# Another load order and other priorities for a fused retention and squared-ReLU FFN kernel

## The chip, the cores and the metric

The kernel runs on one core of a Trainium2 chip. The metric is the device time of one execution in microseconds. Before the change three runs gave 211.70, 212.27 and 212.51 us, so a median of 212.27 us; the profiled execution has a span of 210.5 us from its first to its last instruction.

The names of the engines: PE is TensorE (PEld its weight loads), DVE is VectorE, ACT is ScalarE, POOL is GpSimd, SP is SyncE, which issues nearly all DMAs here.

## The reference, cut to what matters

There are 4 sequences of 768 tokens, 8 heads of 64. A retention recurrence is run over q, k and v, and its output, laid out as 3072 tokens of 512 features, goes through an FFN with 2048 hidden units and a squared ReLU.

```python
gamma = 1.0 - 2.0 ** (-5.0 - np.arange(H))
scale = 1.0 / np.sqrt(D)
for t in range(S):
    state = gamma[None, :, None, None] * state + np.einsum('bhd,bhe->bhde', k[:, :, t], v[:, :, t])
    y[:, :, t] = scale * np.einsum('bhd,bhde->bhe', q[:, :, t], state)
...
x = y.transpose(0, 2, 1, 3).reshape(B * S, H * D)      # 3072 x 512
h = np.maximum(x @ w_in, 0.0)                          # w_in 512 x 2048
return h * h @ w_out                                   # w_out 2048 x 512
```

Inputs and output are float32. The kernel computes the matmuls in bfloat16 with float32 sums.

## The kernel before

The tokens are worked on as 24 tiles of 128. The recurrence is done in chunks: masked scores of a chunk with itself, plus the state of the chunks before, which is carried in bfloat16 and updated by a sum per chunk. The first four tiles are done as two **pairs** (tiles 0 and 1, tiles 2 and 3), whose q, k and v are loaded with 256 tokens each; the later tiles have loads of their own.

The program is not written in the order in which it is issued. Every operation (a load, a cast, a group of matmuls, an eviction) is first added to a `Plan` with its engine, an assumed duration, what it reads and writes, and a priority. Then the plan is run as a list schedule: of all operations whose inputs are there, the one that can start first is placed, and of those that can start at the same time the one with the lowest priority number. The order found so is fixed in the program; the chip keeps to it on each engine and waits where the model was wrong.

```python
best = None
for eng, cand in pool.items():
    for i in cand:
        t = max(eng_free[eng], ready_at[i])
        ...                                    # PSUM banks
        key = (t, o["prio"], i)
        if best is None or key < best[0]:
            best = (key, i, eng)
```

The model of a load has a pipe with a cost per load[...]:

```python
RING = 198; FETCH = 2.6; BLOCK0 = 193; BLOCK = 256; AHEAD = 50      # of class Plan
...
if any(before < x <= issued for x in range(self.BLOCK0 - self.AHEAD, issued + 1, self.BLOCK)):
    behind = [x for x in moves if x[0] > t + 0.4]
    y = max(behind[0][1] if behind else pipe, t + 0.4) + 1.27
    ...                                        # the loads behind it land later
```

The parameters that the plan takes (cut to those that the text speaks of):

```python
SMALL = (1.20, 0.93, 65, 0.6)    # load of a tile: ..., descriptors 65
TWIN = (1.20, 1.80, 65, 0.6)     # load of a pair
BLOCKS = [2, 2, 1, 1, 2, 2, 2, 4, 4, 4]     # tiles in a block of the FFN's first matmul
AHEAD = 4        # how many tiles ahead the loads and casts are added to the plan
WARM = 20.0      # fill matmuls are put in gaps of TensorE up to about this time
PACE = 5; LEAD = 2
NPE = 6; NTD = 7 # tiles 6 to NTD - 1 are turned with 64 x 64 transposes on TensorE, later ones by DMA
PRE = 20         # tiny matmuls at the very start
WHALF = 2        # the first two quarters of w_in come in halves: pieces i0 to i3; then i4, i5
F2LAG = 4.0; F2WAIT = 4
HOME = {...}     # operations that are tied to one engine
RANK = {...}     # priorities set by hand
ORDER = "k0 q0 v0 q2 k2 i0 v2 o0 k4 i1 o1 ..."
```

In the list of loads, `k2` is the k of the tile (or pair) that begins with tile 2, `i0` the first piece of w_in, `o0` the first of w_out. The place in the list is the priority of the load:

```python
dma_prio = {x: n for n, x in enumerate(dma_order(NM))}
```

The weights are loaded as float32 into four staging buffers and cast to bfloat16 from there; w_in and w_out share them, and the pieces of w_in are added to the plan before those of w_out:

```python
pieces = {"in": [(j, h, 2) for j in range(WHALF) for h in range(2)] + [(j, 0, 1) for j in range(WHALF, 4)],
          "out": [(j, 0, 1) for j in range(4)]}

def weights(kind, n):
    j, half, parts = pieces[kind][n]
    slot = (j if kind == "in" else 4 + j) % NWS            # NWS = 4
    ...
    held = [f"wst{slot}.{half}"] if parts == 2 else [f"wst{slot}.0", f"wst{slot}.1"]
    pl.add(f"ldw{kind}{n}", "SP", WHALFD if parts == 2 else WIDE, (), held, ..., prio=dma_prio[(kind, n)])
    for c in range(0, 4, parts):
        pl.add(f"cw{kind}{n}.{c}", WCAST, 0, held, [...], ..., prio=WPRIO[kind] + j)
```

A pair is loaded, cast (`c`), its v scaled (`cv`, on VectorE or GpSimd, line 452), turned (`T`, `E`), scored (`A`, masked by `P`), summed into the state (`B`, line 512, `S`) and applied (`C`, lines 522 and 533; `Y` writes the result to `xt`). B of a pair waits for both halves of its scaled v. Later tiles have `visit(m, n)`, which applies tile m and scores tile n in one group (lines 686, 701, 712, 723). Its priority on TensorE:

```python
prio=-300 + n if m is None else -300 + m if m < PACE else (m - LEAD) * 8
```

The FFN's first matmul (line 835), relu and square (lines 840 and 845), and second matmul (line 880):

```python
pl.add(f"F1.{blk}.{f0}", "PE", ..., prio=blk0[blk] * 8 + 2 * f0 * nb / 4, ...)
pl.add(f"F2.{q4}.{j}",   "PE", ..., prio=(q4 + F2LAG) * 8 + 2 * j + 1 + part * 9, ...)
```

A tile is turned on TensorE or by a DMA transpose (line 660):

```python
if m < 2 * NPAIR or NPE <= m < NTD:
    return                                       # flips(t) in a visit: line 642, then one eviction on ScalarE
if m >= NPE:
    pl.add(f"X{m}", "SP", TURN, ..., lambda: nc.sync.dma_start_transpose(...), prio=-0.5)
    return
```

At the very start and in early gaps TensorE is given work without use[...]:

```python
for _ in range(PRE):
    nc.tensor.matmul(fps[NBANK - 1][0:1, 0:1], lhsT=one, rhs=one, start=True, stop=True)          # line 932
for i in sequence:
    for _ in range(o.get("fill", 0)):
        nc.tensor.matmul(fps[o["fill_bank"]][:, 0 : 2 * P], lhsT=ident[:], rhs=..., ...)          # line 936
```

Of the kernel before, what the change touches and what calls it, by code (L numbers as in the profile page):

```python
# [18 lines left out]
class Plan:  # L19
# [12 lines left out]
    BLOCK = 256  # L32
    AHEAD = 50
    HOP = 0.15
# [6 lines left out]
    def add(self, name, eng, dur, reads=(), writes=(), fn=None, prio=0.0, lat=0.0, bank=None, after=(), count=0):  # L41
# [17 lines left out]
        else:  # L59
            flex = True  # L60
        if name in HOME:
            eng = {HOME[name]: eng[HOME[name]]}
        prio = RANK.get(name, prio)
        self.ops.append(dict(i=i, name=name, eng=eng, flex=flex, deps=sorted(deps), fn=fn,
# [3 lines left out]
    def schedule(self, nbanks, max_open):  # L68
# [18 lines left out]
        if "PE" in eng_free:  # L87
            eng_free["PE"] = 0.06 * PRE
        bank_free = [0.0] * nbanks
# [7 lines left out]
        done = 0  # L97
        issued, edge, next_fetched, history, crossed = 2 * PRE, self.BLOCK0, 3.0, [], 0.0
        while done < n:
# [54 lines left out]
            else:  # L154
                if eng == "PE":
# [9 lines left out]
                    while issued + todo > edge:  # L165
                        step = max(0, edge - issued)
                        now = max(now + step * per, next_fetched)
                        issued, todo = max(issued, edge), todo - step
                        ahead = next((y for x, y in reversed(history) if x <= edge - self.AHEAD), 0.0)
                        ahead = max(ahead, crossed)  # L170
# [5 lines left out]
                    history.append((issued, t + dur))  # L176
                    if any(before < x <= issued for x in range(self.BLOCK0 - self.AHEAD, issued + 1, self.BLOCK)):
                        behind = [x for x in moves if x[0] > t + 0.4]
# [37 lines left out]
STORE = (0.30, 0.80, 9, 0.6)  # L216
BLOCKS = [2, 2, 1, 1, 2, 2, 2, 4, 4, 4]
SPLIT = 6
AHEAD = 4
WARM = 20.0  # L220
FILL = 0.215
WARMING = 18.4
PACE = 5
LEAD = 2
NPE = 6
NTD = 7
PRE = 20
WHALF = 2
WHALFD = (0.60, 1.47, 33, 0.6)
CVT = {'DVE': 0.69, 'POOL': 1.3}  # L230
TCAST = {'DVE': 0.43, 'ACT': 0.63, 'POOL': 0.78}
TEVAC = {'ACT': 0.6, 'DVE': 0.62}
NPAIR = 2
F2LAG = 4.0
F2WAIT = 4
LAST = [256, 128, 128]
CAST = {"k": {"DVE": 0.43, "ACT": 0.63, "POOL": 0.78}, "q": {"DVE": 0.43, "ACT": 0.63, "POOL": 0.78}}
# [2 lines left out]
WPRIO = {"in": -2.0, "out": 2.0}  # L240


HOME = {'cq2.1': 'POOL', 'Eq2.0': 'DVE', 'cq0.1': 'ACT', 'cwout3.3': 'ACT', 'cwin2.0': 'DVE', 'cwin0.0': 'ACT', 'ck2.0': 'ACT', 'ck5': 'DVE', 'Eq4': 'DVE', 'Eq0.1': 'ACT', 'cq4': 'ACT', 'cwin1.2': 'ACT', 'ck6': 'DVE', 'Ek0.0': 'DVE', 'cwout2.3': 'DVE', 'cwin1.0': 'ACT', 'cwin3.2': 'DVE', 'Ek4': 'ACT', 'cwout0.3': 'DVE', 'cq0.0': 'DVE', 'ck4': 'POOL', 'cwin5.2': 'ACT', 'cwout0.1': 'DVE', 'cwout3.1': 'DVE', 'cwout1.3': 'DVE', 'cwout1.0': 'DVE', 'cwout0.2': 'DVE'}
ROUND = []
RANK = {'Ek0.0': -98.1}
ORDER = (
    "k0 q0 v0 q2 k2 i0 v2 o0 k4 i1 o1 i2 q4 o2 i3 o3 i4 v4 i5 q5 q6 q7 k5 v5 v6 k6 k7 v7"
)


# [8 lines left out]
def kernel(  # L259
# [346 lines left out]
    def prepare(m):  # L606
        if m < 2 * NPAIR:
            if m % 2 == 0:
                together(m // 2)
            return  # L610
        b, i = where(m)
        slot = m % NLD
        for x in "kqv":
            t = ld[x][:, slot, :]
            pl.add(f"ld{x}{m}", "SP", SMALL, (), (f"ld{x}{slot}",),
                   lambda x=x, t=t: nc.sync.dma_start(  # L616
                       t.rearrange("s (h d) -> s h d", h=H),
                       src[x][b, :, i * C : (i + 1) * C, :].rearrange("h s d -> s h d")),
                   prio=dma_prio[(x, m)])
        for x in "kq":  # L620
            t, o = ld[x][:, slot, :], bf[x][m % NBF]
            pl.add(f"c{x}{m}", CAST[x], 0, (f"ld{x}{slot}",), (f"bf{x}{m % NBF}",),
                   lambda on, t=t, o=o: copy_on(on, o.rearrange("s j a d -> s a j d"),
                                                t.rearrange("s (a j d) -> s a j d", a=2, j=NJ)), prio=urgency(m))
        t, o = ld["v"][:, slot, :], bf["v"][m % NBF]
        pl.add(f"cv{m}", "DVE", 0.69, (f"ldv{slot}", "vf"), (f"bfv{m % NBF}",),
               lambda: nc.vector.tensor_tensor(  # L627
                   out=o[:], in0=t.rearrange("s (h d) -> s h d", h=H),
                   in1=vf[:, i, :, None].to_broadcast([P, H, D]), op=ALU.mult),
               prio=urgency(m))  # L630
# [21 lines left out]
    def transpose(m):  # L652


        qkT, t = qkts[m % NQT], kq[m % NBF]
# [3 lines that stand above are left out]
            pl.add(f"X{m}", "SP", TURN, (f"bfk{m % NBF}", f"bfq{m % NBF}"), qkeys(m),  # L659
                   lambda: nc.sync.dma_start_transpose(out=qkT.rearrange("p x j t -> p (x j) t"),  # L660
                                                       in_=t.rearrange("s x j a d -> s (x j a d)")), prio=-0.5)
            return
        for x, name in enumerate("kq"):
            o1 = {}

            def fn(x=x, o1=o1):
                ps = fps[o1["op"]["bank_index"]].bitcast(BF16)
                for j in range(NJ):
                    nc.tensor.transpose(ps[:, j * P : j * P + P], t[:, x, j].rearrange("s a d -> s (a d)"), ident[:])
            i0 = pl.add(f"T{name}{m}", "PE", 0.26, (f"bf{name}{m % NBF}", "ident"), (f"gT{name}{m}",), fn,  # L670
                        prio=-200 + m, lat=0.2, count=4, bank=("open", ("T", m, x), False))
            o1["op"] = pl.ops[i0]
            pl.add(f"E{name}{m}", EVAC, 0, (f"gT{name}{m}",), (qkeys(m)[x],),
                   lambda on, x=x, o1=o1: copy_on(on, qkT[:, x].rearrange("p j t -> p (j t)"),
                                                  fps[o1["op"]["bank_index"]].bitcast(BF16)[:, 0:512]),
                   prio=urgency(m), lat=0.05, bank=("close", ("T", m, x)))
# [50 lines left out]
    def visit(m, n, t=None):  # L727
# [28 lines left out]
        if n is None:  # L756
            dur += 0.2
        pl.add(f"V{'' if m is None else m}.{'' if n is None else n}", "PE", dur, reads, writes, fn,
               prio=-300 + n if m is None else -300 + m if m < PACE else (m - LEAD) * 8, lat=0.25,
               count=32 * ((m is not None) + (n is not None) + (t is not None)) + 1)  # L760
# [99 lines left out]
    def ffn2(blk):  # L860
        for q4 in range(blk0[blk], blk0[blk] + blocks[blk]):
# [5 lines left out]
            for part, w in enumerate(widths):  # L867
# [5 lines left out]
                for j in range(4):  # L873
                    reads = [f"h{g % NH2}.{u}.{4 * j + c}" for c in range(4)] + [f"wout{j}.{c}.{h}" for c in range(4) for h in range(2)]

                    def mm(j=j, o1=o1, h2=h2, u=u, ns=ns, w=w):
                        ps = fps[o1["op"]["bank_index"]]
                        for c in range(4):
# [3 lines left out]
                    i0 = pl.add(f"F2.{q4}.{j}" + f"/{part}" * (parts > 1), "PE", 0.866 * w / DM, reads, (f"g{grp}",), mm,  # L882
                                prio=(q4 + F2LAG) * 8 + 2 * j + 1 + part * 9, lat=0.2,
                                bank=("open", grp, True) if j == 0 else ("use", grp), count=4)
# [18 lines left out]
    for m in range(-1, NM):  # L903
        n = m + 1
        for x in range(0 if m < 0 else m + AHEAD, min(NM, m + AHEAD + 1)):
            prepare(x)
            transpose(x)
        t = m + 2 if NPE <= m + 2 < NTD else None
        if n < 2 * NPAIR:
# [18 lines left out]
    if tc is not None:  # L928
        with tc.manual_schedule():
            one = nc.const_aps.tensor(1.0, [P, 1], BF16)  # L930
            for _ in range(PRE):
                nc.tensor.matmul(fps[NBANK - 1][0:1, 0:1], lhsT=one, rhs=one, start=True, stop=True)
# [37 lines left out]
```

## Time and profile before

| What | Value |
|---|---|
| Time, median of 3 | 212.27 us |
| Span of the profiled execution | 210.5 us |
| Line 835, the FFN's first matmul | 90.6 us busy, x637 |
| Line 880, the FFN's second matmul | 86.0 us busy, x395 |
| Line 701, state applied | 10.1 us busy, x296 |
| HBM read, written | 27.26 MB, 6.29 MB |
| Loads of a pair (q, k or v) | 512 KB each, two of each |
| Loads of a tile (q, k or v) | 256 KB each, twenty of each |
| Pieces of w_in | four of 512 KB, two of 1024 KB |
| Pieces of w_out | four of 1024 KB |
| DMA transposes | 17, 4.7 us to landing |

The page gives busy time, shares and counts of each engine; the same in 40 slices of the span; the chain of work that ended last; and the costliest groups. A line of the timeline reads: start and length in microseconds, engine, line of the kernel, operation with the buffer written and the buffer read, how many; in brackets the idle time of the engine just before and what ended it. "SPq" is SyncE issuing a DMA: the length is that of the issue and not of the transfer. In a table of stretches each engine has its busy microseconds and its count of instructions, and then come the granted clock of TensorE (1.00 is full), the mean share of the DMA engines and GB/s.

### The profile page before, as it was taken

What the parts mean: (1) busy time and instruction counts of PE and PEld (TensorE: products, weight loads), DVE (VectorE), ACT (ScalarE), POOL (GpSimd) and SP (SyncE); (2) the same over time, 40 slices, a digit from 0 to 9 for tenths busy, and PEclk for the clock granted to TensorE, in tenths of its full rate; (3) what the DMA queues carried; (4) which work ended last, traced back from release to release, by engine and by line L of the source; (5) the groups of instructions that cost most, each with busy time, mean ns of one, the idle gap of its engine ahead of it and who ended that gap; (6) DMA issues with size and microseconds to landing.
All of it is one profiled execution on the core that took longest, in us unless ns stands there. A gap on an engine that the chain in (4) does not pass through costs nothing.

```text
span 210.5 us, 6029 instructions
## 1 busy us (share of the span) xinstructions
PE 198.0 (94%) x2603; PEld 119.4 (57%) x2627; DVE 115.3 (55%) x252; ACT 89.0 (42%) x150; POOL 39.5 (19%) x67
## 2 busy tenths in 40 slices
PE   7686999999998998999999999999999999999994
PEld 5454888854575856877545444444454444444454
DVE  3587689843675675695713769536786324222000
ACT  8464586644141533543311364412653235444121
POOL 6443222421221122131221222112300000000000
PEclk9998799999999999999999999999999999999999
DMA  6999999999999999999999999299931110110212
GB/s 161 290 300 312 345 369 328 367 206 215 191 239 196 239 175 201 233 181 223 200 204 223 226 181 219 78 218 198 218 50 53 53 50 0 50 50 5 100 50 100
DMA packets 95642, 38.40 MB, mean 182 GB/s; under 512 B 81024, under 2 KB 89600, under 8 KB 95616
## 3 DMA queue, kind: packets, MB, share of 16 engines
q1 hardware_dynamic: 95472, 37.95, 82.1%
q8 instruction: 20, 0.33, 0.7%
q10 hardware_dynamic: 144, 0.07, 0.1%
q14 instruction: 6, 0.05, 0.1%
HBM read 27.26 MB, written 6.29 MB: 159 GB/s over the span
## 4 chain that ended last, share of the span: by engine, by line
PE 61%; DMA 17%; SPq 15%; DVE 3%; issue 2%; POOL 1%; ACT 0%; POOLq 0%
PE fps L880 29%; PE fps L835 27%; SPq L616 8%; DMA vn<-in_v_dram 6%; DMA wst<-in_moe_w_out_dram 5%; SPq L809 5%; DMA qn<-in_q_dram 3%; DMA qkT<-kqs 3%; PE yy L686 2%; PE yy L701 1%; SPq L436 1%; SPq L660 1%; PE sc L712 1%; PE sc L723 1%; DVE pt L766 1%
## 5 line engine op out<-in xcount | busy, mean ns | idle before, releaser
L835 PE MATMUL fps<-xt,w_in 128*128 128x256 bf16 (+2 forms) x637 | 90.6, 296 | 0.3
L880 PE MATMUL fps<-w_out,h 128*128 128x512 bf16 (+2 forms) x395 | 86.0, 362 | 2.1 <-issue 1.6
L840 ACT ACTIVATE h<-fps 128x512 bf16<-128x512 f32 x96 | 57.3, 597 | 57.8 <-PE fps L835 57.2
L835 PEld LDWEIGHTS <-w_in 128*128 128x128 bf16 x640 | 57.3, 99 | 28.7 <-ACT w_in L417 0.3
L845 DVE TENSOR_TENSOR h<-h 128x512 bf16<-128x512 bf16 x96 | 43.1, 461 | 37.4 <-ACT h L840 36.7
L880 PEld LDWEIGHTS <-h 128*128 128x128 bf16 x416 | 38.1, 98 | 39.3
L888 ACT ACTIVATE osb<-fps 128x512 f32<-128x512 f32 (+2 forms) x26 | 14.7, 564 | 48.8 <-PE fps L880 47.7
L788 DVE TENSOR_TENSOR xt<-yy,yf 128x512 bf16<-128x512 f32 x20 | 13.7, 687 | 20.0 <-PE yy L701 20.0
L421 POOL CAST kqs<-kn 128x512 bf16<-128x512 f32 x18 | 11.5, 641 | 55.7 <-DMA kn<-in_k_dram 39.8
L627 DVE TENSOR_TENSOR vs<-vn,vf 128x512 bf16<-128x512 f32 x20 | 14.6, 732 | 10.2 <-DMA vn<-in_v_dram 10.0
L421 POOL CAST kqs<-qn 128x512 bf16<-128x512 f32 x19 | 12.4, 651 | 30.5 <-DMA qn<-in_q_dram 30.5
L779 DVE TENSOR_TENSOR state<-sc,state 128x256 bf16<-128x256 f32 x33 | 13.8, 420 | 0.5
L766 DVE TENSOR_TENSOR pt<-sc,cmask 128x512 bf16<-128x512 f32 x20 | 13.6, 681 | 0.3 <-PE sc L723 0.3
L701 PE MATMUL yy<-qkT,state 64*64 64x64 bf16 x296 | 10.1, 197 | 0.2
L686 PEld LDWEIGHTS <-vs 64*64 64x64 bf16 x320 | 4.2, 107 | 7.3 <-issue 6.3
L712 PE MATMUL sc<-qkT 64*64 64x64 bf16 x320 | 6.2, 194 | 1.6 <-DMA qkT<-kqs 1.6
L936 PE MATMUL fps<-ident 128*128 128x256 bf16 x31 | 6.4, 358 | 0.3 <-POOL ident L352 0.3
L686 PE MATMUL yy<-pt,vs 64*64 64x64 bf16 x320 | 6.4, 198 | 0.3 <-DVE pt L766 0.3
L701 PEld LDWEIGHTS <-state 64*64 64x64 bf16 x296 | 6.2, 107 | 0.5 <-PE yy L701 0.4
L723 PE MATMUL sc<-vs,kqs 64*64 64x64 bf16 x288 | 6.2, 193 | 0.0
L712 PEld LDWEIGHTS <-qkT 64*64 64x64 bf16 x320 | 4.5, 109 | 2.1 <-DMA qkT<-kqs 1.8
L421 POOL CAST w_in<-wst 128x512 bf16<-128x512 f32 x5 | 3.6, 718 | 9.8 <-DMA wst<-in_moe_w_in_dram 9.8
(69 smaller groups left out, 84.6 us busy)
## 6 DMA issues: line engine op xcount, KB each, us to landing
out_dram<-osb SPq DMA_DIRECT2D x23, 256.0 KB, 3.1
kn<-in_k_dram SPq DMA_DIRECT2D x20, 256.0 KB, 5.7
qn<-in_q_dram SPq DMA_DIRECT2D x20, 256.0 KB, 5.1
vn<-in_v_dram SPq DMA_DIRECT2D x20, 256.0 KB, 4.9
wst<-in_moe_w_out_dram SPq DMA_DIRECT2D x4, 1024.0 KB, 10.3
wst<-in_moe_w_in_dram SPq DMA_DIRECT2D x4, 512.0 KB, 7.0
wst<-in_moe_w_in_dram SPq DMA_DIRECT2D x2, 1024.0 KB, 8.9
kn<-in_k_dram SPq DMA_DIRECT2D x2, 512.0 KB, 5.8
```

Of the source, the lines that this page charges most:

```text
L421: nc.gpsimd.tensor_copy(o, t)
L616: lambda x=x, t=t: nc.sync.dma_start(t.rearrange("s (h d) -> s h d", h=H), src[x][b, :, i * C : (i + 1) * C, :].rearrange("h s d -> s h d")),
L627: lambda: nc.vector.tensor_tensor(out=o[:], in0=t.rearrange("s (h d) -> s h d", h=H), in1=vf[:, i, :, None].to_broadcast([P, H, D]), op=AL ...
L686: nc.tensor.matmul(yy[L * c : L * c + L, sub, p * L : p * L + L], lhsT=vs[r, 4 * a + j, :], rhs=pt[r, a, j, :], start=(p == 0), stop=True, ...
L701: nc.tensor.matmul(yy[L * c : L * c + L, sub, p * L : p * L + L], lhsT=st[r, j, :], rhs=qkT[r, 1, j, sub * L : sub * L + L], start=False, ...
L766: lambda: nc.vector.tensor_tensor(out=pt[:], in0=sc[:, :, 0:256].rearrange("s g (p t) -> s g p t", p=NJ), in1=cmask[:, None, None, :].to_b ...
L779: f = lambda cc=cc, j1=j1, j0=j0: nc.vector.tensor_tensor(out=sts[j1][:], in0=cc, in1=sts[j0][:], op=ALU.add)
L835: nc.tensor.matmul(ps[:, u * n : u * n + n], lhsT=w_in_bf[j][:, cb, c * P : (c + 1) * P], rhs=xt[:, cb, cols], start=(cb == 0), stop=(cb = ...
L840: nc.scalar.activation(h2[:, f0 : f0 + per, cols], ps[:].rearrange("p (u n) -> p u n", u=per), AF.Relu)
L845: nc.vector.tensor_mul(hv, hv, hv)
L880: nc.tensor.matmul(ps[:, 0:w], lhsT=h2[:, fb, u * C : u * C + C], rhs=w_out_bf[j][:, c, ns], start=(fb == 0), stop=(fb == NFB - 1))
L888: lambda o1=o1, slot=slot, ns=ns, w=w: nc.scalar.activation(osbs[slot][:, ns], fps[o1["op"]["bank_index"]][:, 0:w], AF.Copy),
```

## The change

The change touches only parameters of the plan: the list of loads, where some operations live, a few priorities and constants. What is computed stays the same. By its own description the list comes from a search[...], and it puts the halves of w_in behind the second pair.

```diff
-AHEAD = 4
+AHEAD = 5
-PACE = 5
-LEAD = 2
+PACE = 10
+LEAD = 1
-NTD = 7
-PRE = 20
+NTD = 8
+PRE = 50
-F2LAG = 4.0
+F2LAG = 5.0
-HOME = {'cq2.1': 'POOL', 'Eq2.0': 'DVE', 'cq0.1': 'ACT', 'cwout3.3': 'ACT', 'cwin2.0': 'DVE', 'cwin0.0': 'ACT', ... 27 in all}
+HOME = {'cq7': 'ACT', 'ck7': 'DVE', 'ck4': 'ACT', 'cwout0.1': 'POOL', 'cwin1.0': 'ACT', 'cq0.0': 'DVE', ... 27 in all}
-RANK = {'Ek0.0': -98.1}
+RANK = {'P0.00': -1.1, 'Tk2.1': 21.9, 'vf20': -1.1, 'B0': 1.9, 'S1': 0.9, 'Y2.0': 5.65}
 ORDER = (
-    "k0 q0 v0 q2 k2 i0 v2 o0 k4 i1 o1 i2 q4 o2 i3 o3 i4 v4 i5 q5 q6 q7 k5 v5 v6 k6 k7 v7"
+    "k0 q0 v0 k2 o0 q2 o1 v2 i0 i1 o2 i2 k4 i3 i4 i5 q4 v4 k5 q5 o3 q6 k6 v5 q7 v6 v7 k7"
 )
```

More of the change, by code (lines that the diff above doesn't have):

```diff
@@ L240 @@
 WPRIO = {"in": -2.0, "out": 2.0}
-HOME = {'cq2.1': 'POOL', 'Eq2.0': 'DVE', 'cq0.1': 'ACT', 'cwout3.3': 'ACT', 'cwin2.0': 'DVE', 'cwin0.0': 'ACT', 'ck2.0': 'ACT', 'ck5': 'DVE', 'Eq4': 'DVE', 'Eq0.1': 'ACT', 'cq4': 'ACT', 'cwin1.2': 'ACT', 'ck6': 'DVE', 'Ek0.0': 'DVE', 'cwout2.3': 'DVE', 'cwin1.0': 'ACT', 'cwin3.2': 'DVE', 'Ek4': 'ACT', 'cwout0.3': 'DVE', 'cq0.0': 'DVE', 'ck4': 'POOL', 'cwin5.2': 'ACT', 'cwout0.1': 'DVE', 'cwout3.1': 'DVE', 'cwout1.3': 'DVE', 'cwout1.0': 'DVE', 'cwout0.2': 'DVE'}
+HOME = {'cq7': 'ACT', 'ck7': 'DVE', 'ck4': 'ACT', 'cwout0.1': 'POOL', 'cwin1.0': 'ACT', 'cq0.0': 'DVE', 'Ek2.0': 'DVE', 'cwout2.0': 'ACT', 'ck2.1': 'POOL', 'cwin5.3': 'DVE', 'ck5': 'ACT', 'cq6': 'ACT', 'Eq5': 'ACT', 'cwin3.0': 'ACT', 'ck6': 'DVE', 'cwout1.0': 'DVE', 'ck0.0': 'DVE', 'cwin4.0': 'DVE', 'cwout3.3': 'ACT', 'cwin1.2': 'DVE', 'cwin5.0': 'DVE', 'Ek0.1': 'ACT', 'cwout1.2': 'POOL', 'cwin2.0': 'ACT', 'cwout0.2': 'DVE', 'cwin4.2': 'DVE', 'cwin5.2': 'POOL'}
 ROUND = []
-RANK = {'Ek0.0': -98.1}
+RANK = {'P0.00': -1.1, 'Tk2.1': 21.9, 'vf20': -1.1, 'B0': 1.9, 'S1': 0.9, 'Y2.0': 5.65}
 ORDER = (
-    "k0 q0 v0 q2 k2 i0 v2 o0 k4 i1 o1 i2 q4 o2 i3 o3 i4 v4 i5 q5 q6 q7 k5 v5 v6 k6 k7 v7"
+    "k0 q0 v0 k2 o0 q2 o1 v2 i0 i1 o2 i2 k4 i3 i4 i5 q4 v4 k5 q5 o3 q6 k6 v5 q7 v6 v7 k7"
 )
```

## The prediction

> **What bounds the kernel now.** I read the busy shares and the 40 slices of the page first, because a schedule change can only win where the bounding engine is not fed.
>
> ```profile
> PE 198.0 (94%) x2603; PEld 119.4 (57%) x2627; DVE 115.3 (55%) x252; ACT 89.0 (42%) x150; POOL 39.5 (19%) x67
> PE   7686999999998998999999999999999999999994
> PEclk9998799999999999999999999999999999999999
> DMA  6999999999999999999999999299931110110212
> ```
>
> The reader is to see three things. TensorE is the bound: it is full from the fifth slice on (one slice is 210.5 / 40 = 5.26 us). It is short of work only in the first four slices, about 21 us. And the fifth slice has a dip in the granted clock. The DMA engines are full, but for one dip, up to slice 29 and nearly idle from slice 31 on (158 us), when TensorE still has 50 us of matmuls to do, so the loads do not set the end; they set only when TensorE can begin.
>
> Next I cut the start into stretches (columns: TensorE busy, weight loads, VectorE, ScalarE, GpSimd, clock, DMA share, GB/s).
>
> ```profile
> 0.00:5.00 5.00, 3.93 (x36) 2.94 (x37) 1.41 (x20) 4.24 (x7) 3.38 (x15) 1.00 0.57 154
> 10.00:15.00 5.00, 4.11 (x108) 2.70 (x107) 4.24 (x9) 2.63 (x6) 2.77 (x5) 1.00 1.17 307
> 15.00:20.00 5.00, 3.06 (x86) 2.29 (x86) 3.89 (x8) 1.65 (x4) 2.10 (x2) 0.99 1.17 303
> 20.00:25.00 5.00, 4.92 (x56) 3.80 (x57) 3.36 (x8) 2.98 (x6) 1.49 (x2) 0.67 1.11 346
> 25.00:30.00 5.00, 5.00 (x76) 4.31 (x74) 4.21 (x10) 3.76 (x7) 0.87 (x1) 1.00 1.07 365
> 21.00:22.00 1.00, 1.00 (x9) 0.63 (x10) 0.94 (x3) 0.16 (x1) 0.85 (x1) 0.50 1.11 346
> ```
>
> Much of the early "busy" is not work at all: the warm-up matmuls on the identity (line 936, x31, 6.4 us busy in the page) and the 20 tiny ones of line 932. The same cut beyond 20 us gives TensorE 175.55 of 180 us busy between 20 and 200, so only about 4.5 us of idle is spread over the whole rest, 1.6 us of it the ten drains of 0.16 us in front of line 880. After the last matmul, at 207.65, only the last eviction and store follow (2.9 us). The time is therefore: the moment at which TensorE gets unbroken work, plus a nearly fixed 186 us of it, plus 2.9 us.
>
> That moment is found in the timeline.
>
> ```profile
> 6.81 1.74 SPq L809 DMA_DIRECT2D wst<-in_moe_w_in_dram  x1
> 8.59 0.86 SPq L436 DMA_DIRECT2D vn<-in_v_dram  x1
> 12.30 0.63 ACT L417 ACTIVATE h<-kn 128x512 bf16<-128x512 f32 x1 [1.02 <-DMA kn<-in_k_dram]
> 13.85 0.62 POOL L421 CAST w_in<-wst 128x512 bf16<-128x512 f32 x1 [0.90 <-DMA wst<-in_moe_w_in_dram]
> 15.63 1.05 PE L835 MATMUL fps<-xt,w_in 128*128 128x256 bf16 x8
> 16.96 1.55 POOL L452 TENSOR_TENSOR h<-vn,vf 128x512 bf16<-128x512 f32 x1 [2.49 <-DMA vn<-in_v_dram]
> 18.56 0.60 PE L512 MATMUL fps<-h 64*64 64x64 bf16 x32 [1.66 <-POOL h L452]
> 20.52 0.72 PE L533 MATMUL yy<-qkT,state 64*64 64x128 bf16 x8
> 21.17 2.97 PE L835 MATMUL fps<-xt,w_in 128*128 128x256 bf16 x16
> ```
>
> The first half of w_in (i0) is issued at 6.81, ahead of the v of the second pair (v2) at 8.59. i0 lands at 13.85, but only 8 matmuls are made of it (15.63). Then TensorE waits 1.66 us, because v2 landed at 16.96 and GpSimd's half of its scaling takes 1.55 us. The rest of the second pair ends at about 21.2, and from there TensorE runs through.
>
> [...] the clock is 0.97 in the stretch 19 to 20, 0.50 in the three after it and 0.82 from 23 to 24, so 1.7 us of clock are lost in about 3.5, right behind the idle 1.66 us. [...] the first 18 identity matmuls take 4.02 us (223 ns each, 256 columns) and five later ones 0.71[...]. [...] the trace has 20 such packets with 0.33 MB on its instruction queue q8, one between 12 and 14 us and one between 18 and 20 us. [...]
>
> **The change part by part.** It adds no arithmetic. It moves loads, priorities and the homes of casts.
>
> 1. **Load order.** The list is one of priorities: a load goes when its buffer is free. o0 shares its staging buffer with i0 and i1, o1 with i2 and i3, so the early o0 and o1 of the new list cannot go early; they go when those casts are done, as now (first w_out at 22.53). What really changes at the start: k0 q0 v0 q2 k2 **i0** v2 k4 i1 i2 becomes k0 q0 v0 k2 q2 v2 **i0 i1 i2** k4. The landings of 512 KB pair loads are 1.8 us apart (from 5.09 for k0 to 12.30 for k2 are four of them: 7.21 / 4), and i0 took 13.85 - 12.30 = 1.55 us. So v2 comes 1.5 us earlier at least, at about 15.4. It might be 14.1 (12.30 + 1.8): between i0 and v2 lie 3.1 us where 1.8 would do, and I do not know what took the other 1.3, so I count only 1.5. The chain from v2 to unbroken work is 21.17 - 16.96 = 4.2 us of casts and matmuls, which does not change: 15.4 + 4.2 = 19.6 in place of 21.2. i0 comes at 15.4 + 1.5 = 16.9, i1 at 18.4, i2 at 20. One half gives two blocks of two tiles 8 matmuls each, 2 x 0.9 = 1.8 us (48 such matmuls run in 5.40 us at 24.20), for 1.5 us of load, so TensorE should not starve on them. The 8 matmuls at 15.63 are still done before 19.6, in the gap. **-1.5 us.**
>
> 2. **The half-speed window.** It costs the 1.7 us just summed, nearly all on TensorE's path. With 1.5 us less waiting in front of it, it may not come. I give that 4 in 10: **-0.7 us.**
>
> 3. **PRE 20 to 50.** 30 more tiny matmuls at 0.64 / 20 = 0.032 us: 1 us more, ending near 2.4 us, in front of data that lands at 5.09. **0.** [...]
>
> 4. **NTD 7 to 8.** Tile 7 is turned on TensorE like tile 6 (line 642, 32 small transposes, 0.27 us to the next group at 50.40) and a DMA transpose goes, 17 to 16. ScalarE gets one eviction of 1.02 us beside its 42%. **+0.3 us**, of which a shorter wait for a transpose could return 0.1.
>
> 5. **PACE 10, LEAD 1, F2LAG 5.** Retention visits of tiles 5 to 9 are now placed as soon as the model has their data, later ones closer to their use, the second matmul of the FFN one tile later. TensorE runs in order, so a visit placed too early is a wait. Now there are two waits for a transposed tile, 1.6 us together, and one of 0.3 for the masked scores. I allow **+0.3 us** more.
>
> 6. **HOME.** The casts of weights change engine; one lasts 0.43 us on VectorE, 0.63 on ScalarE, 0.62 to 0.87 on GpSimd. None of these engines is over 55% busy. **0.**
>
> Sum: 212.27 - 1.5 - 0.7 + 0.3 + 0.3 = **210.7 us**.
>
> **The rivals.**
>
> First: **the wait moves**. v2 comes sooner but w_in later, and TensorE waits for w_in in place of v2. For it: 4 MB of w_in need about 12 us at the 346 GB/s of 20 to 25 us, and before tiles 4 and 5 are there four tiles give the eight halves of w_in just 8 x 1.8 = 14 us of matmuls, a thin margin; in the new order k4, q4 and v4 also come behind more of w_in, so the visit of tile 4, at 29.53 now, cannot fill holes. Against it: matmuls need only the half that has landed. If it happens, the 1.5 us are used up and the time is 212 to 213.
>
> Second: **the clock decides**. If the half-speed window goes and v2 lands at 14.1, the gain is 1.7 + 2.8, less 0.6 for steps 4 and 5, and the time is about 208.4. If a second such window appears, because fill matmuls were placed by a model whose landings were off (as with the 1.66 us wait now, which nothing filled), it is 1.7 us the other way, about 212.5.
>
> Third: **the list misses in the middle**. If visits of tiles 5 to 9 are early by a load time each (median 4.9 to 5.7 us from issue to landing) TensorE collects several waits of 0.5 to 1 us, between 45 and 100 us, where the DMA is full: +2 to 3 us, 213 to 214. Against it: TensorE has a large stock of FFN work there, and the four retention lines (686, 701, 712, 723) are only 28.9 of its 198 us.
>
> Fourth: **nothing**, the start is hidden by later waits for loads. Against it stands the DMA row: loads end well ahead of TensorE.
>
> **Range and chances.** The core is 210.7; the good rival leads to 208.3, the bad ones to 213.5. The range 208.4 to 213.4 should hold 8 in 10. Faster by over 2% means under 208.0: it needs the clock window and the early v2 together, 0.1. Slower by over 2% means above 216.5, more waits than any view suggests: 0.05. Within 2%: 0.85.
>
> **What would show each step.** Step 1: the scaling of v2 on line 452 starts at 14 to 15.5 in place of 16.96, and line 835 runs through from 19 to 20. Step 2: no stretch at 0.5 between 15 and 25, a sum of lost clock below 1.7 us. Step 4: line 642 counts 64 matmuls and line 660 has 16 transposes. Step 5: TensorE's waits on transposed tiles and masked scores stay below 2.5 us in all. It would be wrong if line 835 waits for w_in's casts between 17 and 30, if a new dip of the clock appears, or if TensorE's idle between 45 and 100 grows by more than 1 us.

## The result and the profile after

The changed kernel takes 210.5 us (median of 4 runs, 210.27 to 210.59) against 212.17 us before on the same chip: a ratio of 0.9921 with a 95% interval of 0.99 to 0.9942. The prediction was 210.7 us. The span of the profiled execution went from 210.5 to 208.5 us.

First the lines of the page after that answer to those of the page before (busy shares; the 40 slices of TensorE, of its clock and of the DMA engines, a slice now 5.21 us):

```profile
PE 196.3 (94%) x2660; PEld 118.8 (57%) x2687; DVE 112.9 (54%) x249; ACT 91.2 (44%) x154; POOL 39.8 (19%) x67
...
PE   7667999998999999999999999999999999999994
...
PEclk9999999999999999999999999999999999999999
DMA  5999999999998999999999999979920110011212
```

TensorE is still the bound, still short of work in four slices, and the DMA engines still finish some 50 us before it. The dip of the clock is gone from this execution, but not from the kernel: of its four timed runs one, the profiled one, has a mean clock of 1.000, and three have 0.992, which is as much as the dip before took (0.008 of 208.7 us, 1.7 us). The stretches of the start say how little else changed there (columns as before: TensorE, weight loads, VectorE, ScalarE, GpSimd, clock, DMA share, GB/s):

```profile
15.00:20.00 5.00, 3.26 (x70) 2.54 (x70) 3.19 (x7) 1.75 (x3) 2.10 (x2) 1.00 1.14 320
20.00:25.00 5.00, 4.86 (x83) 3.77 (x82) 4.09 (x9) 3.39 (x7) 1.23 (x2) 1.00 1.06 379
...
21.00:22.00 1.00, 0.93 (x30) 0.58 (x27) 1.00 (x4) 0.97 (x2) 0.00 (x0) 1.00 1.05 380
```

From 15 to 20 us TensorE is busy for 3.26 us in place of 3.06. The timeline of the changed kernel has the rest:

```profile
15.61 1.55 POOL L452 TENSOR_TENSOR h<-vn,vf 128x512 bf16<-128x512 f32 x1 [2.74 <-DMA vn<-in_v_dram]
15.74 0.25 PE L496 MATMUL sc<-qkT 64*64 64x128 bf16 x4 [1.38 <-issue]
...
17.05 0.63 ACT L417 ACTIVATE w_in<-wst 128x512 bf16<-128x512 f32 x1 [2.12 <-DMA wst<-in_moe_w_in_dram]
...
17.99 1.05 PE L835 MATMUL fps<-xt,w_in 128*128 128x256 bf16 x8
...
18.57 0.43 DVE L419 CAST w_in<-wst 128x512 bf16<-128x512 f32 x1 [1.12 <-DMA wst<-in_moe_w_in_dram]
18.91 0.98 DVE L580 TENSOR_TENSOR state<-fps,state 128x256 bf16<-128x256 f32 x2
...
21.90 1.05 PE L835 MATMUL fps<-xt,w_in 128*128 128x256 bf16 x8
...
23.01 8.02 PE L835 MATMUL fps<-xt,w_in 128*128 128x256 bf16 x72
```

The v of the second pair (v2) is scaled from 15.6 on in place of 16.96, and the first half of w_in (i0) is cast from 17.05 in place of 13.85. But the second pair is not ready sooner: VectorE sits 1.12 us in front of a cast of the second half (i1, 18.57) and only then adds the states (18.91), so the pair ends at 22 us. Up to then TensorE has made two groups of 8 FFN matmuls, one at 17.99 and one at 19.26, where the kernel before had made one. Unbroken work begins at 21.90 us in place of 21.17, so it is not an earlier start of it that saves the time.

Two sums account for most of the 2.0 us of span. **By 40 us** lines 835 and 880 together were busy for 19.3 us after (15.55 + 3.75) and for 19.4 us before (18.00 + 1.37), but of the latter the 16 matmuls at 21.17 took 2.97 us in place of the 1.8 us that they take at full clock (72 such matmuls run in 8.02 us at 23.01 above); so the changed kernel is about 1.1 us of FFN ahead. **After 40 us** the waits of TensorE with a releaser were 1.6 and 0.3 us before and are 0.4 and 0.4 us after, 1.1 us less. These are the lines, first of the kernel before, then of the kernel after (what waited, for what: us in total, times, longest):

```profile
PE sc L712 <- DMA qkT<-kqs: 1.6, 2, 0.9
...
PE yy L686 <- DVE pt L766: 0.3, 1, 0.3
```

```profile
PE fps L835 <- DVE xt L788: 0.4, 1, 0.4
PE sc L723 <- DVE vs L627: 0.4, 1, 0.4
```

1.1 + 1.1, less 0.3 for the turning of tile 7 on TensorE and 0.3 for the drains in front of line 880 (1.9 us in place of 1.6), is 1.6 of the 2.0 us. This is where the time lies in one pair of profiles. Read alone, it would put the first 1.1 us down to the clock and the second to tile 7; the experiments bear out neither.

### The profile page after: what moved, and what is told of

Same layout as the page of the kernel before. It is cut to its first block, busy times and chain, and to the rows that moved or that the text cites. A ratio compares the mean times of both kernels' runs of the same rounds, so it can differ in the third digit from the quotient of the medians.

```text
span 208.5 us, 6143 instructions
## 1 busy us (share of the span) xinstructions
PE 196.3 (94%) x2660; PEld 118.8 (57%) x2687; DVE 112.9 (54%) x249; ACT 91.2 (44%) x154; POOL 39.8 (19%) x67
## 4 chain that ended last, share of the span: by engine, by line
PE 73%; DMA 16%; SPq 5%; issue 2%; POOL 1%; ACT 1%; DVE 1%; ACTq 0%
PE fps L880 35%; PE fps L835 31%; DMA wst<-in_moe_w_out_dram 5%; DMA wst<-in_moe_w_in_dram 4%; DMA vn<-in_v_dram 4%; DMA qn<-in_q_dram 3%; SPq L809 3%; PE yy L686 2%; SPq L436 2%; PE yy L701 1%; PE sc L723 1%; PE sc L712 1%; SPq L616 1%; POOL w_out L421 1%; ACT qkT L648 0%
## 5 line engine op out<-in xcount | busy, mean ns | idle before, releaser
L835 PE MATMUL fps<-xt,w_in 128*128 128x256 bf16 (+2 forms) x635 | 87.4, 293 | 0.9 <-DVE xt L788 0.4
L880 PE MATMUL fps<-w_out,h 128*128 128x512 bf16 (+2 forms) x394 | 84.3, 362 | 2.4 <-issue 1.9
L845 DVE TENSOR_TENSOR h<-h 128x512 bf16<-128x512 bf16 x96 | 41.8, 447 | 33.6 <-ACT h L840 33.3
L421 POOL CAST kqs<-kn 128x512 bf16<-128x512 f32 x16 | 10.7, 670 | 64.6 <-DMA kn<-in_k_dram 55.7
L627 DVE TENSOR_TENSOR vs<-vn,vf 128x512 bf16<-128x512 f32 x20 | 14.3, 716 | 3.2 <-DMA vn<-in_v_dram 3.2
L421 POOL CAST kqs<-qn 128x512 bf16<-128x512 f32 x17 | 10.8, 633 | 22.8 <-DMA qn<-in_q_dram 22.8
L421 POOL CAST w_out<-wst 128x512 bf16<-128x512 f32 x6 | 4.4, 745 | 8.7 <-DMA wst<-in_moe_w_out_dram 8.7
L936 PE MATMUL fps<-ident 128*128 128x256 bf16 x29 | 5.8, 333 | 0.0
```

The source lines that it names most:

```text
L421: nc.gpsimd.tensor_copy(o, t)
L627: lambda: nc.vector.tensor_tensor(out=o[:], in0=t.rearrange("s (h d) -> s h d", h=H), in1=vf[:, i, :, None].to_broadcast([P, H, D]), op=AL ...
L835: nc.tensor.matmul(ps[:, u * n : u * n + n], lhsT=w_in_bf[j][:, cb, c * P : (c + 1) * P], rhs=xt[:, cb, cols], start=(cb == 0), stop=(cb = ...
L845: nc.vector.tensor_mul(hv, hv, hv)
L880: nc.tensor.matmul(ps[:, 0:w], lhsT=h2[:, fb, u * C : u * C + C], rhs=w_out_bf[j][:, c, ns], start=(fb == 0), stop=(fb == NFB - 1))
```

## The experiments

Each was timed beside the kernel before on the same chip. Three chips were used, and on them the kernel before had medians of 211.61, 211.65 and 211.87 us. The theories: **the load order** itself, **the clock** (the half-speed window, which the profile after does not have), **the middle** (fewer waits after 40 us, from NTD and the priorities), and later **the homes** (which engine casts what, in which order, while w_in arrives).

### The list of loads alone

```diff
 # the kernel before
 ORDER = (
-    "k0 q0 v0 q2 k2 i0 v2 o0 k4 i1 ..."
+    "k0 q0 v0 k2 o0 q2 o1 v2 i0 i1 ..."
```

> The kernel before with only the new list of loads; the plan is run anew with the old constants (AHEAD, PACE, LEAD, NTD, PRE, F2LAG, HOME, RANK as before). The theory of the clock: the gain of the start is the half-speed window that does not come, not the earlier v2. It expects v2 near 15.5 (in place of 16.96), and then, if TensorE is busier from 16.5 to 20, a clock of 1.00 throughout and 0.7 to 1.0% less than before; if the half-speed window still comes, within 0.3% of before, although v2 is early. The rival, the load order itself (step 1 of the prediction): 0.7% less even where the clock dips. The rival of the middle: the gain comes from constants that act after 40 us, and then this run is within 0.3% of before.

Measured: 211.25 us, ratio 0.9989 (0.9978 to 0.9999). v2 was scaled from 13.96 us on, 3 us sooner than before, and the gain is 0.2 us. The clock dipped in this profile as well (0.54, 0.50, 0.50 and 0.75 in the stretches from 18 to 22). TensorE now waits for i0:

```profile
13.96 1.04 POOL L452 TENSOR_TENSOR h<-vn,vf 128x512 bf16<-128x512 f32 x1 [0.60 <-DMA vn<-in_v_dram]
...
17.53 1.39 PE L835 MATMUL fps<-xt,w_in 128*128 128x256 bf16 x8 [1.11 <-ACT w_in L417]
```

The load order by itself brings next to nothing.

### Filling the gap of the kernel before

```diff
+                if o["name"] == "B2":
+                    o["fill"], o["fill_bank"] = 14, o["bank_index"]
                 for _ in range(o.get("fill", 0)):
```

> The kernel before with its order of instructions untouched, and 14 identity matmuls (256 columns) put in front of the B group of tile 2, where TensorE waited 1.66 us for the scaled v2 at 16.9. Loads, casts and matmuls of use keep their order. The theory of the clock: no stretch at 0.5 from 20 to 23.6, and 1.3 to 1.7 us less, 0.6 to 0.8% (210.5 to 211). The rival, the load order: the wait is the same, so the time is too, within 0.2%[...].

Measured: 211.39 us, ratio 0.9983 (0.9961 to 1.0004). The window is gone, in the profile and in 20 of the 22 runs (mean clock 0.998 or more). In the stretches of this kernel:

```profile
21.00:22.00 1.00, 1.00 (x10) 0.67 (x8) 0.85 (x2) 0.07 (x1) 0.72 (x1) 1.00 1.12 356
```

The clock is 1.00 where it was 0.50, and the matmuls of line 835 that ended at 29.6 us end at 28.3. Yet the time hardly moves: the theory of the clock expected 1.3 to 1.7 us and got 0.2 to 0.4. The order of the matmuls of use is the same in both kernels, so they can be compared one by one: the lead is 1.3 us at 28 us, 0.8 at 36, 0.5 at 42 and 0.2 at 46, so most of it is lost while the rest of w_in and the first of w_out arrive. (In this pair of profiles it is 0.9 us again from 54 us on, where the kernel before has more waits.)

The runs of the kernel before say much the same. Sorted by their mean granted clock, 150 of them are: 39 above 0.995, median 211.67 us; 72 near 0.992, 211.80 us; 39 near 0.984 (twice the loss), 211.43 us. The window comes in three runs of four (111 of 150), and over the three chips no cost of it can be seen. On the second chip alone it looks otherwise: ten runs with twice the loss have a median of 212.41 us, eight with none 211.33 us.

### The list, with its gap filled

```diff
 # the kernel before with the new list
+                if o["name"] == "F1.0.0":
+                    o["fill"], o["fill_bank"] = 10, o["bank_index"]
```

> The kernel before with the new list of loads, as in the run of the list alone, and 10 identity matmuls in front of the first group of line 835, where TensorE waited 1.11 us for the first half of w_in; nothing else differs. In the run of the list alone the clock stood at half from about 18.4 to 21.3, 1.7 us lost. The theory that list and clock together are the change: without the dip 0.6 to 0.8% below before (209.6 to 210.3), the gain of the changed kernel, without one of its other constants. The rival, that the other constants carry the gain: it stays within 0.3% of before.

Measured: 211.25 us, ratio 0.9978 (0.9962 to 0.9994); 20 of its 22 runs have the full clock, and the median is that of the list alone. Nor do the runs of the list alone differ among themselves: ten with the full clock have a median of 211.25 us, eight near 0.992 also 211.25, four near 0.984 211.28. Two timeline lines show why, first of the list alone, where the clock dipped, then of the list filled, where it did not:

```profile
23.59 7.15 PE L835 MATMUL fps<-xt,w_in 128*128 128x256 bf16 x64
```

```profile
23.51 7.16 PE L835 MATMUL fps<-xt,w_in 128*128 128x256 bf16 x64 [1.06 <-POOL w_in L421]
```

With the full clock TensorE reaches this group more than 1 us sooner and then waits 1.06 us for the cast of the fourth half of w_in (i3). With the dip it comes late and waits for nothing. Here the half-speed window had been taking time in which TensorE would have stood still. This is the first rival of the prediction: the wait moves to w_in.

### One group moved

```diff
 # the list filled
     sequence = pl.schedule(NBANK, 2)
+    at = {o["name"]: o["i"] for o in pl.ops}
+    for a, b in [('F1.0.6', 'F1.1.2'), ('R0.6', 'R1.2'), ('Q0.6', 'Q1.2')]:
+        sequence.remove(at[a])
+        sequence.insert(sequence.index(at[b]) + 1, at[a])
```

> The kernel before with the new list and the 10 identity matmuls, as in the run of the list filled, and one group moved: the first FFN group that needs the fourth half of w_in (F1.0.6, with its relu and square) goes behind two groups of the second block whose halves are there (F1.1.0, F1.1.2), as the changed kernel has them. In the run of the list filled TensorE waited 1.06 us there for a cast of the fourth half. The theory that the order of groups at the arrival of w_in is what the list alone lacks: the wait is gone or under 0.3 us and the time 0.3 to 0.5% lower than there, 0.993 to 0.995 of before. The rival, that TensorE only waits later (for the next pieces of w_in): a new wait of about 1 us between 24 and 35 us and no change, 0.997 to 0.999.

Measured: 211.31 us, ratio 0.9973 (0.9962 to 0.9984): the rival was right. TensorE no longer waits for the cast of i3 but for the second pair's output, which the group of the other block needs. One line of TensorE and two of VectorE, from the timelines of this kernel:

```profile
24.00 3.54 PE L835 MATMUL fps<-xt,w_in 128*128 128x256 bf16 x31 [1.37 <-DVE xt L601]
```

```profile
22.92 0.43 DVE L419 CAST w_in<-wst 128x512 bf16<-128x512 f32 x1 [0.85 <-DMA wst<-in_moe_w_in_dram]
23.27 0.68 DVE L601 TENSOR_TENSOR xt<-yy,yf 128x512 bf16<-128x512 f32 x1
```

VectorE has the second half of the pair's output (line 601) behind a cast of i3 in its queue. It stands in front of that cast for 0.85 us until i3 has landed, and the output comes at 23.9. In the changed kernel the same output is free of it:

```profile
21.67 0.68 DVE L601 TENSOR_TENSOR xt<-sc,yf 128x512 bf16<-128x512 f32 x1
22.27 0.68 DVE L601 TENSOR_TENSOR xt<-yy,yf 128x512 bf16<-128x512 f32 x1
```

There i3 is cast on ScalarE and GpSimd (22.66 and 22.69), and TensorE works on groups of the second block meanwhile: its row of 72 matmuls from 23.01 has no wait.

### The list with the homes, the list with the priorities

```diff
 # the kernel before with the new list, and of the change also
+HOME, RANK, PRE = 50, AHEAD = 5           # first kernel
+PACE = 10, LEAD = 1, F2LAG = 5.0, NTD = 8 # second kernel
```

> The kernel before with the new list, HOME, RANK, PRE and AHEAD of the change; PACE, LEAD, F2LAG and NTD as before. Its order on TensorE is that of the changed kernel up to some 40 us. The theory of the start: 0.5% or more below before (0.995 or less), most of the gain of the changed kernel, whatever the middle does. The theory of the middle: within 0.3% of before.

> The kernel before with the new list, PACE, LEAD, F2LAG and NTD of the change; HOME, RANK, PRE and AHEAD as before. Its order on TensorE is that of the list alone up to some 40 us and another one after it. The theory of the start (homes of casts and ranks decide the order up to 30 us): 0.9975 to 0.999 of before, like the list alone. The theory of the middle: the wait of 0.8 us of line 835 for a tile's output is gone and the gain is 0.5% or more, 0.995 or less.

Measured: with the homes 210.29 us, ratio 0.9933 (0.9912 to 0.9953); with the priorities 212.01 us, ratio 1.0005 (0.9988 to 1.0022). So most of the gain comes with HOME, RANK, PRE and AHEAD, and none with the priorities. The first kernel has the changed kernel's order on TensorE up to some 40 us; its timeline has the same row:

```profile
22.91 8.02 PE L835 MATMUL fps<-xt,w_in 128*128 128x256 bf16 x72
```

With this row it has made 96 matmuls of line 835 by 30.9 us, the list alone 88 by 30.7 us. Eight matmuls take 0.9 us, so the start is worth about 0.7 us. The spans of the two profiles differ by more, 209.3 and 208.0 us, and most of the rest lies in the middle. TensorE's waits there, first of the list alone, then of the list with the homes:

```profile
PE fps L835 <- DVE xt L788: 0.8, 1, 0.8
```

```profile
PE sc L723 <- DVE vs L627: 0.7, 1, 0.7
```

The first wait, at 117.21 us, is also in the list filled and with the group moved, at nearly the same time and length (0.84 us each), and not in the list with the homes. The second, at 48.84 us, has 0.2 us in the list alone. So about 0.7 us of the gain over the list alone is seen at the arrival of w_in; the plan with these constants has another middle as well, and what share of the rest belongs to it was not tested.

In the list with the homes the clock does go with the time: seven runs with the full clock have a median of 209.97 us, eleven near 0.992 210.31, four near 0.984 211.43. Whether the window costs time there, or late loads bring both, was not tested.

The second kernel has the order of the list alone at the start, and no gain. Its middle is not better either: TensorE still waits 0.9 us for transposed tiles.

### Everything but the list

```diff
 # the changed kernel
-    "k0 q0 v0 k2 o0 q2 o1 v2 i0 i1 ..."
+    "k0 q0 v0 q2 k2 i0 v2 o0 k4 i1 ..."
```

> The changed kernel with the old list of loads alone, the plan run anew. The theory that the list is needed: v2 comes behind the first half of w_in again, near 16.9, and the time is that of before within 0.3%. The rival, that the other constants carry the gain: 0.5% or more below before with the old list.

Measured: 212.03 us, ratio 1.0004 (0.9971 to 1.0037). With the old list the other constants together are worth nothing. v2 lands at 16.8, and TensorE waits for its scaling:

```profile
18.44 0.88 PE L512 MATMUL fps<-h 64*64 64x64 bf16 x32 [2.38 <-POOL h L452]
```

So the gain belongs neither to the list alone nor to the rest alone: it needs both. The homes with the old list, without the priorities, were not run.

### Tile 7, both ways

```diff
-NTD = 7
+NTD = 8      # the kernel before; and 8 to 7 in the changed kernel
```

> The kernel before with NTD = 8 alone: tile 7 is turned on TensorE, the DMA transposes are 16. Its order on TensorE is that of before up to its instruction 1366, some 50 us in. The theory of the middle: the two waits of line 712 for transposed tiles (0.86 and 0.77 us) shrink, which together with 0.3 us more of transposes gives 0.2 to 0.6% less. If the waits come from where the visits are placed (PACE, LEAD, F2LAG), not from the transpose of tile 7, the time is within 0.3% or 0.1% more. The dip of the clock from 20 to 23.6 stays.

> The changed kernel with NTD = 7, tile 7 turned by DMA as before; its order on TensorE is that of the changed kernel up to its instruction 1406. The theory of the middle: waits of line 712 for transposed tiles come back (1 to 2 us in all) and 0.2 to 0.6% of the gain is lost. The rival, that tile 7 does not matter: within 0.2% of the changed kernel, 0.991 to 0.993 of before.

Measured: the kernel before with tile 7 on TensorE 211.32 us, ratio 0.9991 (0.997 to 1.0013); the changed kernel with tile 7 by DMA 209.96 us, ratio 0.9902 (0.987 to 0.9934). Tile 7 does not matter in either. In the first the waits of line 712 are gone, as the theory of the middle had it, and the time stays. In the second they do not come back. So the 1.1 us of waits in my account above can't be read as a gain of NTD: the plan is run anew for each kernel, and which waits of half a microsecond it has in the middle differs from one to the next.

The second kernel shows something else. Its order on TensorE is that of the changed kernel up to its instruction 1406, yet in its profile v2 came at 14.00 in place of 15.61. Three lines of it:

```profile
14.00 1.58 POOL L452 TENSOR_TENSOR h<-vn,vf 128x512 bf16<-128x512 f32 x1 [1.17 <-DMA vn<-in_v_dram]
...
18.34 0.43 DVE L419 CAST w_in<-wst 128x512 bf16<-128x512 f32 x1 [0.94 <-DMA wst<-in_moe_w_in_dram]
...
22.17 0.69 DVE L601 TENSOR_TENSOR xt<-yy,yf 128x512 bf16<-128x512 f32 x1
```

A v2 that is 1.6 us earlier makes the pair's last output 0.1 us earlier (22.17, in place of 22.27). VectorE stands in front of its cast of i1 in both, and i1 comes at 18.34 and 18.57: the end of the pair follows i1 and not v2.

### The stall in the middle of a group

```diff
 # the changed kernel: the plan still reckons with 50
-            for _ in range(PRE):
+            for _ in range(20):
                 nc.tensor.matmul(fps[NBANK - 1][0:1, 0:1], lhsT=one, rhs=one, start=True, stop=True)
```

> The changed kernel with its plan and order untouched, but 20 tiny matmuls sent at the start in place of 50, so that every later instruction of TensorE is 60 places earlier[...]. In the changed kernel TensorE stood 1.38 us in the middle of a group of scores (line 496, 12 of 16 done, near its instruction 449), waiting for nothing that the profile shows. The theory that this is a fetch of instructions: the wait is gone from that group at 14.4, and turns up, if at all, 60 instructions later. The theory that it ate the gain of the early v2: 0.4 to 0.7% faster than the changed kernel. The rival, that it was hidden behind the wait for v2 which ends at 17.2: within 0.2% of the changed kernel (0.9921 of before), even if the stall is gone.

Measured: 210.19 us, ratio 0.9921 (0.9896 to 0.9946), the changed kernel's own ratio. The stall of 1.38 us is gone. Two lines of TensorE in this kernel:

```profile
14.00 0.42 PE L496 MATMUL sc<-qkT 64*64 64x128 bf16 x16
...
17.58 1.05 PE L835 MATMUL fps<-xt,w_in 128*128 128x256 bf16 x8 [1.08 <-POOL w_in L421]
```

All 16 scores run at once, v2 came at 14.06, and all but 0.2 us of it is given back at 17.58 and 19.08 in waits for w_in, which lands within 0.2 us of when it did.

### Two versions that might have been faster

```diff
 # the kernel with 20 tiny matmuls
+                if o["name"] in {'F1.0.0': 9, 'F1.0.2': 4}:
+                    o["fill"], o["fill_bank"] = ..., o["bank_index"]
-NTD = 8                                  # in the second version only
+NTD = 7
```

> The changed kernel with 20 tiny matmuls in place of 50, and 9 and 4 identity matmuls in front of the first two groups of line 835, where it waited 1.08 and 0.46 us for w_in. Its runs without the fills fell in two groups, near 209.6 and near 210.6. The theory that the upper group is the half-speed window: only the lower group is left, a median near 209.6, 0.4 us less than without fills and 1.0% less than before. The rival, that the two groups have another cause (the chip, the loads): both groups stay and the median is within 0.15% of that without fills.

> The changed kernel with NTD = 7, 20 tiny matmuls in place of 50, and the 9 and 4 identity matmuls: the three edits that lost nothing, together. If they add up, 209.4 to 209.7 us and 0.987 to 0.990 of before; if the flip of tile 7 helps where the start is faster, no better than the changed kernel with the 20 tiny matmuls and the fills, 0.990.

Measured: the first 209.74 us, ratio 0.9897 (0.9865 to 0.993), the second 210.26 us, ratio 0.9929 (0.9908 to 0.995), each with six runs. Both intervals hold the changed kernel's 0.9921, so neither is shown to beat it, and the edits do not add up. The two groups of times of the kernel with 20 tiny matmuls (209.5 to 209.9 and 210.5 to 211.2, six runs each) are not the clock: in both groups most runs have the full clock. Nor are they the kernel's own work for the most part: four of the six longer runs have a span of 207.8 to 208.3 us from the first to the last instruction, and the shorter ones 207.7 to 207.9, so their extra time lies outside the span. What it is stays open. With the fills five of six runs are near 209.7, too few to tell whether they removed it.

## Why the prediction was right, point by point

**The bound and the place.** Right: TensorE bounds the kernel and the loads' end does not matter. Wrong is the sum built on it, the moment at which unbroken work begins plus a nearly fixed 186 us: that moment came 0.7 us later (21.90 in place of 21.17), and the time fell all the same. In these two profiles that is because TensorE had made one more group of FFN matmuls by then and had the full clock for the next, and because its waits after 40 us were shorter.

**Step 1, the load order, -1.5 us.** The landings were right to 0.2 us: v2 at 15.6 (said 15.4), i0 at 17.05 (16.9), i1 at 18.57 (18.4), i2 at 20.13 (20). For v2 this is luck: with tile 7 by DMA, and in the list alone, it came at 14.0, the other figure that the prediction named. What failed is the sentence that the chain of 4.2 us from v2 to unbroken work "does not change". It took 6.3 us (15.61 to 21.90), and 8.05 with the v2 that came at 14.00 (to 22.05), because VectorE's queue holds casts of w_in between its steps, and they now wait for loads (for i1 1.12 us in the first, 0.94 us in the second). The sign named for this step, line 835 running through from 19 to 20, did not come. The step -1.5 us is refuted as a term of its own: the list alone gave 0.2 us, with v2 at 13.96.

**Step 2, the clock, -0.7 us.** The window is not in the profile, but three of the four timed runs of the changed kernel have one. The term took the 1.7 us of lost clock to be on TensorE's path. It is not where TensorE is ahead of w_in: the list alone has the same median of 211.25 us with and without the dip. For the list with the homes this is not shown. Nor is it shown why the first 18 identity matmuls take 223 ns each and five later ones 142 ns (0.71 / 5): the prediction's row for 0 to 5 us has a granted clock of 1.00.

**Step 4, tile 7, +0.3 us.** The count was right (16 transposes by DMA, 64 matmuls in line 642), and no cost or gain of it could be measured, either way round.

**Step 5, priorities, +0.3 us.** With the list alone they gave 1.0005 where the list alone gave 0.9989, about 0.3 us worse. That agrees, but the two intervals overlap. In the profile it went the other way: between 45 and 100 us TensorE is idle for 1.7 us after and 2.9 us before.

**Step 6, homes, 0.** This is the term that was missed. I read that no engine is over 55% busy and stopped. Together with the ranks, the tiny matmuls and AHEAD the homes make the difference between 0.9989 and 0.9933, about 1.2 us, with the new list, of which about 0.7 us shows in the start; with the old list all constants together make none. A share of busy time doesn't show what stands in front of what in an engine's queue.

So the sum of 210.7 was right by luck, through terms that were partly wrong: -2.2 for steps 1 and 2 stood in for a gain of 1.4 us that comes from the list and the homes together. Of the rivals, "the wait moves to w_in" was the true one for the list alone, where the 1.5 us were used up, as it said, but for 0.2. Which of HOME, RANK, PRE and AHEAD carries the 1.2 us was not taken apart. That it is the home of the casts of i3 is what the timelines of VectorE suggest; moving that one cast was not tried, and PRE has no share that shows (20 in place of 50 left the ratio at 0.9921).

## What to carry to other kernels

A wait that ends early only pays as far as the next arrival on the same path: before pricing an earlier load, list what the engine will need next and when that lands. Where engines keep to a fixed order, look for operations that wait for a load and stand in a queue in front of something that is on the path; moving them to another engine may be worth more than the load order, however idle the engines look (here the moves were tried only together with other constants). Price a change of many constants by groups of constants, since here the list alone gave 0.1%, the homes and all else without the list nothing, and list and homes together 0.7%.

## What the runs showed of the hardware

The granted clock fell to half in or soon after gaps of 1.4 and 1.7 us. The kernel before dips after a single wait of 1.66 us that ends at 18.56 (0.97 from 19 to 20 us, 0.50 from 20 to 23). The changed kernel with tile 7 by DMA dips at the end of a stall of 1.41 us that ends at 15.74 (0.82 from 15 to 16 us, 0.50 from 16 to 19); its matmuls take 0.33 us from 14 to 15 us and 0.26 us from 15 to 16. The same gap does not always bring the dip. Two stretches of that kernel, then the same two of the changed one:

```profile
15.00:16.00 1.00, 0.26 (x5) 0.14 (x4) 0.00 (x0) 0.00 (x0) 0.58 (x1) 0.82 1.10 349
16.00:17.00 1.00, 1.00 (x17) 0.53 (x15) 0.89 (x2) 0.18 (x1) 0.15 (x1) 0.50 1.10 348
```

```profile
15.00:16.00 1.00, 0.26 (x5) 0.19 (x5) 0.44 (x1) 0.00 (x0) 0.39 (x1) 1.00 1.11 352
16.00:17.00 1.00, 0.43 (x3) 0.24 (x4) 1.00 (x3) 0.00 (x0) 1.00 (x1) 1.00 1.10 347
```

With nearly the same stall (1.41 and 1.38 us) and the same 0.26 us of work the clock falls in one execution and stays in the other. What decides between them is not shown.

TensorE stood still inside a group for a reason that no wait names. In the three kernels with 50 tiny matmuls and the new list (the changed one, tile 7 by DMA, list with homes) it stood 1.38 to 1.41 us with 12 of 16 scores done, at its 449th instruction. In the kernels with 20 the stall was not there, nor with 50 and the old list, where the 449th instruction falls into the scores that start at 15.31 us and run through (16 in 0.52 us). That the stall went when all instructions moved by 60 places fits the theory of a fetch of instructions, but does not show it: a packet of the queue that the profile calls "instruction" runs from 13.1 to 14.3 us with 50 tiny matmuls and with 20 alike, and the stall ends at 15.74. Its cost was hidden, for the most part (a ratio of 0.9921 with it and without), because TensorE had to wait for w_in in any case (1.08 and 0.46 us in the kernel with 20).
